# Probabilities as the stationary operand, an unselected phase for the first token tiles, and wider score banks and FFN blocks

## The chip, the cores and the metric

One core of a Trainium2 chip runs the whole program. The metric is the device time of one execution in microseconds (us), as the median of several runs of the same program.

## What is computed

Attention with a choice of key chunks, and a feed-forward block (FFN) behind it. Batch 4, 8 heads, 768 tokens, head size 64; FFN over 3072 tokens, 512 to 2048 to 512, weights in float32.

```python
k_min, k_max = chunk minima and maxima of k       # 24 chunks of 32 keys
ub = sum(max(q * k_min, q * k_max), axis=-1)      # one bound per query and chunk
ub = where(causal by chunk, ub, -1e9)
top_chunks = argsort(ub)[..., -6:]                # six chunks per query
scores = where(chosen and causal, q @ k.T / 8, -1e9)
x = softmax(scores) @ v                           # (3072, 512), heads side by side
h = maximum(x @ w_in, 0)
out = (h * h) @ w_out
```

The first 128 tokens of a batch see four chunks at most, fewer than six, so that nothing is left out for them.

## The kernel before

A *pair* is two heads of one batch; there are 16 pairs, four per batch. Everything is held in SBUF as bf16. GpSimd issues the loads (`load_qk`, `load_v`: two heads of 768 tokens each; `load_w_in`, `load_w_out`), SyncE the stores.

`stage_a` prepares a pair: TensorE (PE) transposes k and q one head at a time (line 188, 64 columns of the array each), VectorE copies them into `kqc` and `qsc` (L198), reduces chunk maxima and minima (L203), and splits q into its positive and negative parts (L215, L216). `selection` multiplies these into the bounds `ub` (L228, L230), finds the sixth largest (L239), marks the chunks that are not chosen (`selb`, L240), turns the marks with PE (`sT`, L248) and copies them below q (L253). The score product then has 88 rows: 64 of q and k, and 24 that subtract 32768 where a chunk is not chosen.

`stage_b` works on a pair and a block of 384 queries. For each key tile of 128 and each head it makes transposed scores `ps` (keys x queries, L378), ScalarE takes the exponential into `e` (L382), and GpSimd zeroes the upper triangle of diagonal tiles (`affine_select`, L385). `values` uses v as the stationary operand, with 64 columns of ones beside its 64 columns, and moves up to 384 columns of `e` through it (L344): half of the output rows are the sums. `finish` takes their reciprocal as exp(-ln) on ScalarE (L358, L361) and VectorE multiplies into `xT` (L368), which is already transposed for the FFN.

Four pairs complete a block of 384 tokens. `ffn_units` cuts its FFN into 16 units `up` (four matmuls of 384 columns into `ph`, L287; relu on ScalarE, L292; square on VectorE, L294) and 12 units `down` (four matmuls of 512 columns into `py`, L301; the last copies out, L306, and stores). `run_ffn` places them between score tiles at a rate per column (`pace`), and a block's units run beside the attention of the next block; after the last pair 144 FFN matmuls stand alone.

The table `phases` lists, block by block, stage A, stage B and the loads; `aside` spreads stage A between key tiles. From the program so written the framework's scheduler makes each engine's list: it moves instructions that are free to go ahead of others, so that the lists differ from the order of the code. Each engine runs its list strictly in order. PSUM is split into one bank for transposes and bounds (`pst`), three for scores, two for values, two for the FFN.

## Time and profile before

| | |
|---|---|
| median of 3 runs | 325.76 us (325.62 to 326.14) |
| span of the profiled execution, first to last instruction | 324.3 us |
| PE busy, 2096 matmuls | 294.6 us, 91% |
| ScalarE (ACT) busy, 548 instructions | 221.1 us, 68% |
| VectorE (DVE) busy, 619 | 207.9 us, 64% |
| GpSimd (POOL) busy, 254 | 110.0 us, 34% |
| chain that ended last, by engine | PE 66%, DVE 17%, ACT 7% |

No time of its own is given for the profiled execution; its span is 1.5 us below the median of the runs. Busy time is the union of the records. A matmul's record lasts from its issue until its result is out, several overlap, and so the busy share of PE says little of how many columns it could still take; the distance between two starts says more.

### The profile page before, as it was taken

To read this page: it belongs to the slowest core of one execution; us is meant where nothing else is said; L and a number is where in the kernel's file an instruction comes from. 1 tells how busy PE (TensorE), PEld (TensorE's weight loads), DVE (VectorE), ACT (ScalarE), POOL (GpSimd) and SP (SyncE) were. 2 spreads that over 40 slices of the span, in tenths; PEclk is the share of its full clock that TensorE was granted. 3 is DMA by queue.
4 is the path that set the end of the run, shared out by engine and by line. 5 is a ranking of instruction groups with operands and counts; after the bars stand their busy time and mean duration, and the time that the engine had idled before them with its cause. 6 is when DMAs were issued, how large, how long until landed. Compare 5 with 4: busy or idle time off the path is not lost.

```text
span 324.3 us, 6103 instructions
## 1 busy us (share of the span) xinstructions
PE 294.6 (91%) x2096; PEld 158.9 (49%) x2096; DVE 207.9 (64%) x619; ACT 221.1 (68%) x548; POOL 110.0 (34%) x254
## 2 busy tenths in 40 slices
PE   1577699999998999999999999999999999999995
PEld 0233345554454555555455545554455555554542
DVE  6775678997799877995576487993675214421420
ACT  6367377984477486887579667787489679973731
POOL 8954754892224733223323212120123211210000
PEclk9999999999999999999999999999999999999999
DMA  9999999999503971333140000000100000001001
GB/s 76 173 179 192 108 199 154 136 145 114 92 0 26 136 102 35 25 24 26 66 59 2 32 34 34 0 2 1 67 33 0 34 33 32 2 0 65 35 32 65
DMA packets 81642, 20.86 MB, mean 64 GB/s; under 512 B 75108, under 2 KB 78028, under 8 KB 81612
## 3 DMA queue, kind: packets, MB, share of 16 engines
q0 software_dynamic: 77616, 13.63, 53.3%
q1 hardware_dynamic: 3996, 6.85, 5.7%
q8 instruction: 16, 0.26, 0.3%
q14 instruction: 14, 0.11, 0.1%
HBM read 27.26 MB, written 6.29 MB: 103 GB/s over the span
## 4 chain that ended last, share of the span: by engine, by line
PE 66%; DVE 17%; ACT 7%; issue 3%; POOL 3%; DMA 2%; POOLq 0%; ACTq 0%
PE py L301 23%; PE ph L287 18%; PE ps L378 9%; DVE xT L368 3%; ACT rc L358 3%; DVE qsc L198 3%; PE kT L188 2%; DMA kn<-in_k_dram 2%; DVE kr L203 2%; PE sT L248 2%; ACT e L382 2%; ACT ht L292 1%; PE qT L188 1%; ACT rc L361 1%; DVE qp L215 1%
## 5 line engine op out<-in xcount | busy, mean ns | idle before, releaser
L382 ACT ACTIVATE e<-ps 128x384 bf16<-128x384 f32 (+2 forms) x288 | 111.4, 431 | 34.7 <-PE ps L378 33.2
L385 POOL TENSOR_SCALAR_AFFINE_SELECT e<-e 128x128 bf16<-128x128 bf16 x192 | 57.0, 305 | 167.4 <-ACT e L382 165.8
L287 PE MATMUL ph<-xT,w_in_sb 128*128 128x384 bf16 x512 | 106.3, 329 | 3.0 <-ACT ht L292 2.7
L378 PE MATMUL ps<-qsc,kqc 88*128 88x384 bf16 (+2 forms) x288 | 72.9, 306 | 3.2 <-ACT e L382 2.7
L292 ACT ACTIVATE ht<-ph 128x384 bf16<-128x384 f32 x128 | 63.8, 505 | 15.4 <-PE ph L287 13.1
L287 PEld LDWEIGHTS <-w_in_sb 128*128 128x128 bf16 x512 | 48.2, 98 | 37.5 <-issue 12.6
L344 PEld LDWEIGHTS <-vo 128*128 128x128 bf16 x288 | 28.4, 101 | 21.6 <-issue 6.2
L378 PEld LDWEIGHTS <-kqc 88*128 88x128 bf16 x288 | 27.4, 101 | 19.4 <-issue 3.3
L198 DVE COPY kqc<-kT 64x768 bf16<-64x768 bf16 (+1 forms) x40 | 19.0, 474 | 25.7 <-PE kT L188 25.3
L203 DVE TENSOR_REDUCE kr<-kT 128x24 bf16<-128x768 bf16 (+1 forms) x40 | 30.4, 792 | 0.3
L306 ACT COPY ob<-py 128x512 f32<-128x512 f32 x24 | 14.1, 586 | 22.0 <-PE py L301 21.8
L253 DVE COPY qsc<-sT 24x640 bf16<-24x640 bf16 (+2 forms) x40 | 16.7, 417 | 4.1 <-PE sT L248 3.3
L85 POOL DMA_DIRECT2D vo<-in_v_dram x16 | 16.5, 1039 | 6.9 <-PE ps L378 6.9
L188 PE MATMUL kT<-ident,kn 128*64 128x128 bf16 x192 | 10.9, 239 | 8.7 <-DMA kn<-in_k_dram 8.2
L198 DVE COPY qsc<-qT 64x768 bf16<-64x768 bf16 (+1 forms) x32 | 16.1, 503 | 3.7 <-PE qT L188 3.3
L75 POOL DMA_DIRECT2D kn<-in_k_dram x16 | 16.6, 1036 | 2.0 <-PE ps L378 1.2
L361 ACT ACTIVATE rc<-rc 128x384 f32<-128x384 f32 x32 | 16.5, 515 | 0.1
L75 POOL DMA_DIRECT2D qn<-in_q_dram x16 | 16.4, 1027 | 0.2
L188 PEld LDWEIGHTS <-kn 128*64 128x64 bf16 x192 | 6.8, 116 | 16.6 <-DMA kn<-in_k_dram 9.0
L248 PE MATMUL sT<-ident,selb 128*128 128x128 bf16 x80 | 8.5, 232 | 4.7 <-DVE selb L240 4.3
L188 PE MATMUL qT<-ident,qn 128*64 128x128 bf16 x192 | 10.3, 237 | 1.3 <-DMA qn<-in_q_dram 1.0
L188 PEld LDWEIGHTS <-qn 128*64 128x64 bf16 x192 | 6.6, 115 | 9.2 <-issue 5.7
(646 smaller groups left out, 470.7 us busy)
## 6 DMA issues: line engine op xcount, KB each, us to landing
out_dram<-ob SPq DMA_DIRECT2D x24, 256.0 KB
kn<-in_k_dram POOLq DMA_DIRECT2D x16, 192.0 KB, 5.2
qn<-in_q_dram POOLq DMA_DIRECT2D x16, 192.0 KB, 5.5
vo<-in_v_dram POOLq DMA_DIRECT2D x16, 192.0 KB, 5.3
w_out_sb<-in_moe_w_out_dram POOLq DMA_DIRECT2D x1, 2048.0 KB, 15.7
w_in_sb<-in_moe_w_in_dram POOLq DMA_DIRECT2D x1, 1536.0 KB, 11.4
kqc<-kqc SPq DMA_DIRECT2D x15, 36.0 KB
w_in_sb<-in_moe_w_in_dram POOLq DMA_DIRECT2D x1, 512.0 KB, 9.4
```

Source lines behind the costliest of these rows:

```text
L75: nc.gpsimd.dma_start(out=nat[nm, b][:, h:h + 2].rearrange("p h j d -> p (h j) d"), in_=src[b, h:h + 2].rearrange("h (j p) d -> p (h j) d" ...
L188: nc.tensor.matmul(pt[D * hh:D * hh + D, 128 * j:128 * (j + 1)], lhsT=nat[nm, b][:, 2 * hp + hh, n0 * HT + j], rhs=ident, is_transpose=Tru ...
L198: nc.vector.tensor_copy(ops[s][hh][0:D, cols], pt[rows])
L203: nc.vector.tensor_reduce(kr[:, mm], pt.rearrange("d (c j) -> d c j", j=CH), axis=AX.X, op=op)
L287: nc.tensor.matmul(ph, lhsT=w_in_sb[:, ki, 128 * f:128 * (f + 1)], rhs=xT[:, ki], start=(ki == 0), stop=(ki == NKI - 1))
L292: nc.scalar.activation(ht, ph, ACT.Relu)
L301: nc.tensor.matmul(py, lhsT=h2[f][:, 128 * t:128 * (t + 1)], rhs=w_out_sb[:, f, :], start=(f == 0), stop=(f == NFI - 1))
L344: nc.tensor.matmul(hold["av"][hh][:, off:], lhsT=vo[b % 2].rearrange("p h n d -> p (h n d)")[:, c0:c0 + 2 * D], rhs=es[hh][:, off:], start ...
L361: nc.scalar.activation(rc, rc, ACT.Exp, scale=-1.0)
L378: nc.tensor.matmul(ps[:, off:], lhsT=kq[s][hh][:, 128 * j:128 * (j + 1)], rhs=qs[s][hh][:, q0 + off:q1], start=True, stop=True)
L382: nc.scalar.activation(e[:, off:], ps[:, off:], ACT.Exp, scale=scale)
L385: nc.gpsimd.affine_select(out=e[:, off:off + 128], in_=e[:, off:off + 128], compare_op=ALU.is_ge, fill=0.0, base=0, channel_multiplier=-1, ...
```

## The change

The queries of the first tile of every batch leave the selection. A new phase at the start (`first_transpose`, `first_scores`, `first_values`) handles the tile (0, 0) of all heads of all four batches: 64-row scores without marks, exponential, triangle, values. Its result `x_first` is an FFN block of 512 tokens. The other 640 tokens of a batch are one block, whose `up` units go in halves of 320 columns. There are five blocks instead of eight.

Scores are packed: per head and pair five PSUM banks of 512 columns (`BANKS`), each filled by two products of the 15 tiles below and the five on the diagonal; one exponential covers a bank. `values` takes each 128 x 128 tile of `e` as the stationary operand and moves 65 columns of v through it (64 and a column of ones), so that the output has queries as rows; `normalise` divides by the 65th column on VectorE. Hence x must be transposed for the FFN: `turn`, four PE transposes and a VectorE copy per tile.

k and q of both heads are transposed at once (128 columns of the array), q without its first tile, and q is copied by ScalarE. Loads go by token tile over all eight heads. At the end of every batch the queue `behind` and the remaining FFN units are drained. Four sets of `kqc`/`qsc` instead of eight; six buffers of `e` (of 512) instead of twelve (of 384).

```diff
+    QC = 128 * NS
+    VW = 80
+    NSET = 4
+    LAG = 3
...
-    epool = ctx.enter_context(tc.tile_pool(name="epool", bufs=12))
-    hpool = ctx.enter_context(tc.tile_pool(name="hpool", bufs=NFI + 8))
+    epool = ctx.enter_context(tc.tile_pool(name="epool", bufs=LAG + 3))
+    hpool = ctx.enter_context(tc.tile_pool(name="hpool", bufs=NFI + 6))
...
-    psav = ctx.enter_context(tc.tile_pool(name="psav", bufs=1, space=PSUM))
+    psav = ctx.enter_context(tc.tile_pool(name="psav", bufs=2, space=PSUM))
...
+    def load_first(nm, b0, b1):
...
+            out=dst.rearrange("p b h d -> p (b h) d"),
+            in_=SRC[nm][b0:b1, :, 0:128].rearrange("b h p d -> p (b h) d"))
...
+    def load_rest(nm, b, j):
...
+        nc.gpsimd.dma_start(
+            out=nat[nm, b][:, j - 1, :, 0:D],
+            in_=SRC[nm][b, :, 128 * j:128 * (j + 1)].rearrange("h p d -> p h d"))
...
+    load_first("k", 0, 2)
     ident = consts.tile([128, 128], BF16, tag="ident")
     make_identity(nc, ident)
-    load_qk(0, "q")
-    load_qk(1)
+    load_first("q", 0, 2)
+    load_first("v", 0, 2)
+    load_first("k", 2, 4)
+    load_first("q", 2, 4)
+    load_first("v", 2, 4)
+    load_w_in(0, 4)
...
+    for nm in "kq":
+        for j in range(1, NT):
+            load_rest(nm, 0, j)
+    load_w_in(4, 8)
...
+    def causal(e, n):
+        nc.gpsimd.affine_select(
+            out=e, in_=e, compare_op=ALU.is_ge, fill=0.0, base=0,
+            channel_multiplier=-1, pattern=[[0, n], [1, 128]])
+    def normalise(av, n, x):
+        rc = work.tile([128, NS], F32, tag="rc", name="rc")
+        nc.vector.reciprocal(rc[:, 0:n], av[:, :, D])
+        nc.vector.tensor_mul(
+            x, av[:, :, 0:D],
+            rc[:, 0:n].unsqueeze(2).to_broadcast([128, n, D]))
+    x_first = work.tile([128, B, d_model], BF16, tag="x0", name="x0", bufs=1)
+    t_first = {}
+    e_first = {}
+    def first_transpose(b):
+        pt = pst.tile([128, 2, NP, 128], BF16, tag="tp", name="T0")
+        for i, nm in enumerate("kq"):
+            for hp in range(NP):
+                nc.tensor.matmul(pt[:, i, hp], lhsT=key_tile(nm, b, hp, 0),
+                                 rhs=ident, is_transpose=True,
+                                 start=True, stop=True)
+        t_first[b] = work.tile([128, 2, NP, 128], BF16, tag="t0", name="t0")
+        nc.vector.tensor_copy(t_first[b], pt)
+    def first_scores(b):
+        t = t_first.pop(b)
+        es = []
+        for hh in range(2):
+            rows = slice(D * hh, D * hh + D)
+            ps = pss.tile([128, NP, 128], F32, tag="ps", name="ps0")
+            for hp in range(NP):
+                nc.tensor.matmul(ps[:, hp], lhsT=t[rows, 0, hp],
+                                 rhs=t[rows, 1, hp], start=True, stop=True)
+            e = epool.tile([128, NP, 128], BF16, tag="e", name="e0")
+            nc.scalar.activation(e, ps, ACT.Exp, scale=scale)
+            causal(e, NP)
+            es.append(e)
+        e_first[b] = es
+    def first_values(b):
+        es = e_first.pop(b)
+        for hh in range(2):
+            av = psav.tile([128, NP, D + 1], F32, tag="av", name="av0")
+            for hp in range(NP):
+                nc.tensor.matmul(av[:, hp], lhsT=es[hh][:, hp],
+                                 rhs=value_tile(b, 2 * hp + hh, 0),
+                                 start=True, stop=True)
+            normalise(av, NP, x_first[:, b].rearrange(
+                "p (hp hh d) -> p hp hh d", hh=2, d=D)[:, :, hh])
...
+        pt = pst.tile([128, S], BF16, tag="tp", name="kT")
+        for j in range(NT):
+            nc.tensor.matmul(pt[:, 128 * j:128 * (j + 1)],
+                             lhsT=key_tile("k", b, hp, j), rhs=ident,
+                             is_transpose=True, start=True, stop=True)
...
+        pt = pool.tile([128, QC], BF16, tag=tag, name="qT")
+        for j in range(1, NT):
+            nc.tensor.matmul(pt[:, 128 * (j - 1):128 * j],
+                             lhsT=key_tile("q", b, hp, j), rhs=ident,
+                             is_transpose=True, start=True, stop=True)
...
+        for hh in range(2):
+            nc.scalar.copy(qss[0:D, s, hh], pt[D * hh:D * hh + D])
...
+    def ffn_units(x, rows, parts):
...
+        def turn(t):
+            pt = psf.tile([128, NKI, 128], BF16, tag="ff", name="xt")
+            for ki in range(NKI):
+                nc.tensor.matmul(pt[:, ki], lhsT=x[:, t, 128 * ki:128 * (ki + 1)],
+                                 rhs=ident, is_transpose=True,
+                                 start=True, stop=True)
+            nc.vector.tensor_copy(xT[:, :, 128 * t:128 * (t + 1)], pt)
...
-                    rhs=xT[:, ki],
+                    rhs=xT[:, ki, c0:c1],
...
+        for t in range(n):
+            units.append((0.25, lambda t=t: turn(t)))
         for f in range(NFI):
-            units.append((tb, lambda f=f: up(f)))
+            for c0, c1 in parts:
+                units.append(((c1 - c0) / 512, lambda f=f, c0=c0, c1=c1:
+                              up(f, c0, c1)))
...
+    BANKS = [
+        ([(0, 1, 2), (1, 1, 2)], (2, 3)),
+        ([(2, 2, 1), (0, 3, 3)], (0, 1)),
+        ([(4, 4, 1), (1, 3, 3)], (0, 1)),
+        ([(5, 5, 1), (3, 3, 3)], (0, 2)),
+        ([(4, 5, 1), (2, 3, 3)], None),
+    ]
...
+    def values(p, hh, i, e, x):
...
+        for n, (j, t0, nt) in enumerate(BANKS[i][0]):
+            for t in range(t0, t0 + nt):
+                nc.tensor.matmul(
+                    av[:, t - 1], lhsT=e[:, 128 * c:128 * (c + 1)],
+                    rhs=value_tile(b, 2 * hp + hh, j),
+                    start=(i == 0 and c == 0), stop=(i == len(BANKS) - 1),
+                    skip_group_check=True)
...
+        if i == len(BANKS) - 1:
+            h = 2 * hp + hh
+            normalise(held.pop("av"), NS, x[:, :, D * h:D * (h + 1)])
...
+        for hh in range(2):
+            for i, (runs, diagonal) in enumerate(BANKS):
+                ps = pss.tile([128, 512], F32, tag="ps", name="ps")
+                c = 0
+                for j, t0, nt in runs:
+                    nc.tensor.matmul(
+                        ps[:, 128 * c:128 * (c + nt)],
+                        lhsT=kqs[:, s, hh, 128 * j:128 * (j + 1)],
+                        rhs=qss[:, s, hh, 128 * (t0 - 1):128 * (t0 - 1 + nt)],
+                        start=True, stop=True)
+                    c += nt
+                e = epool.tile([128, 512], BF16, tag="e", name="e")
+                nc.scalar.activation(e, ps, ACT.Exp, scale=scale)
+                if diagonal:
+                    d0, d1 = diagonal
+                    causal(e[:, 128 * d0:128 * d1].rearrange(
+                        "p (n j) -> p n j", j=128), d1 - d0)
+                run_ffn()
+                behind.append(lambda p=p, hh=hh, i=i, e=e, x=x:
+                              values(p, hh, i, e, x))
+                if len(behind) > LAG:
                     behind.pop(0)()
...
+    first_transpose(0)
+    first_transpose(1)
+    first_scores(0)
+    first_transpose(2)
+    first_scores(1)
+    first_values(0)
+    first_transpose(3)
+    first_scores(2)
+    first_values(1)
+    first_scores(3)
+    first_values(2)
+    first_values(3)
+    ffn.extend(ffn_units(x_first, [S * b for b in range(B)], [(0, 512)]))
...
+    loads(6)
+    aside.append((0, stage_a(0)))
+    for p in range(B * NP):
+        b, hp = divmod(p, NP)
+        if hp == 0:
+            x = work.tile([128, NS, d_model], BF16, tag="x", name="x")
+            pace["rate"] = sum(u[0] for u in ffn) / (10 * NP)
+        finish_a(p)
+        if p + 1 < B * NP:
+            aside.append((p + 1, stage_a(p + 1)))
+        loads(8)
+        stage_b(p, x)
+        if hp == NP - 1:
+            while behind:
+                behind.pop(0)()
+            while ffn:
+                ffn.pop(0)[1]()
+            pace["due"] = 0.0
+            ffn.extend(ffn_units(
+                x, [S * b + 128 * t for t in range(1, NT)],
+                [(0, QC // 2), (QC // 2, QC)]))
```

On GpSimd, this is the start of the list before (`kn`, `qn`, `vo` are k, q, v of two heads).

```order
L75 DMA kn<-in_k_dram 128x12x64
masks.py:197 MEMSET ident 128x128
L75 DMA qn<-in_q_dram 128x12x64
...
L85 DMA vo<-in_v_dram 128x12x64 x2
L385 AFFINE_SELECT e<-e 128x128 x12
L156 DMA w_in_sb<-in_moe_w_in_dram 128x4x1536
```

And now (`k_86`, `q_87`, `v_88` are first tiles, `e_178` to `e_288` their probabilities, `kn`, `qn`, `vn` the other tiles).

```order
L74 DMA k_86<-in_k_dram 128x16x64
...
L103 DMA w_in_sb<-in_moe_w_in_dram 128x4x512
L151 MEMSET ubmask 128x120
...
L86 DMA qn<-in_q_dram 128x8x64 x5
L103 DMA w_in_sb<-in_moe_w_in_dram 128x4x512
L168 AFFINE_SELECT e_178<-e_178 128x512
...
L168 AFFINE_SELECT e_288<-e_288 128x512
L83 MEMSET vn 128x40
L86 DMA vn<-in_v_dram 128x8x64 x2
L103 DMA w_in_sb<-in_moe_w_in_dram 128x4x1024
L86 DMA vn<-in_v_dram 128x8x64 x3
L108 DMA w_out_sb<-in_moe_w_out_dram 128x8x512 x2
L86 DMA kn<-in_k_dram 128x8x64 x5
L86 DMA qn<-in_q_dram 128x8x64
L168 AFFINE_SELECT e<-e 128x128 x3
```

Before, the first select stood behind 13 loads; now 18 loads stand ahead of the first tiles' selects, and 14 more between these and the first select of pair 0.

On ScalarE, the start of the list before, and now.

```order
L196 COPY qsc<-qT 64x384 x4
L382 ACTIVATE e<-ps 128x384 x2
L382 ACTIVATE e<-ps 128x256 x2
L382 ACTIVATE e<-ps 128x128 x2
L196 COPY qsc<-qT 64x384 x2
```

```order
L205 ACTIVATE e_280<-ps_275 128x512
L205 ACTIVATE e_288<-ps_283 128x512
L254 COPY qsc<-qT 64x640 x2
L405 ACTIVATE e<-ps 128x512 x6
L320 ACTIVATE ht<-ph 128x512
L254 COPY qsc<-qT 64x640 x2
L320 ACTIVATE ht<-ph 128x512 x7
L405 ACTIVATE e<-ps 128x512 x7
```

The first relu of the FFN (`ht`) now stands behind eight exponentials of the first tiles, the q copies of pair 0 and six of its banks.

On PE, the place of the first score product before (`kn` transposes of pair 2 and bounds of pair 1 around it), and the end of the first phase now (`e_178` holds probabilities of the first tiles, `qn` is the rest of q of pair 0).

```order
L188 MATMUL kT<-ident,kn 64x128
L378 LDWEIGHTS kqc
L378 MATMUL ps<-qsc,kqc 128x384
L228 LDWEIGHTS qp
L228 MATMUL ub<-kbd,qp 128x48
```

```order
L227 MATMUL kT<-ident,kn 128x128
L246 LDWEIGHTS qn
L246 MATMUL qT<-ident,qn 128x128
...
L215 LDWEIGHTS e_178
L215 MATMUL av_216<-v_88,e_178 128x65
```

The transposes of k and q of pair 0 stand behind the first tiles' scores and ahead of their values, where before pairs 0 to 2 went through their first halves one after the other. The first `ph` product now stands behind nine banks of `ps`.

## Rows read from the trace of the kernel before

**Rows 1.** Busy time by stretches: us, then each engine (count), clock, DMA share, GB/s.
```profile
0.00:45.00 45.00, 27.45 (x167) 13.42 (x168) 30.59 (x107) 24.84 (x56) 30.06 (x61) 1.00 1.53 150
45.00:150.00 105.00, 100.91 (x830) 55.30 (x829) 92.01 (x282) 76.70 (x196) 50.14 (x97) 1.00 1.00 84
150.00:290.00 140.00, 135.63 (x947) 75.23 (x946) 78.49 (x213) 106.22 (x272) 29.81 (x97) 1.00 0.11 26
290.00:324.30 34.30, 30.62 (x156) 14.98 (x154) 6.84 (x18) 13.34 (x26) 0.00 (x0) 1.00 0.12 47
```

**Rows 2.** The chain that ended last, from 296 us: start us, length us, what.
```profile
299.08 0.65 PE ph L287 x4
...
299.76 10.53 PE ph L287 x60
310.29 10.37 PE py L301 x48
...
320.68 0.58 ACT ob L306
```

**Rows 3.** PE in order of time, two places past 49 us: start us, length us, what.
```profile
49.96 0.22 PE L344 MATMUL av_709<-e,vo 128*128 128x128 bf16 x1
50.02 0.22 PE L344 MATMUL av_710<-e,vo 128*128 128x128 bf16 x1
...
93.11 0.53 PE L188 MATMUL qT<-ident,qn 128*64 128x128 bf16 x12
93.57 2.51 PE L287 MATMUL ph<-xT,w_in_sb 128*128 128x384 bf16 x13
...
96.24 0.19 PE L228 MATMUL ub<-kbd,qp 128*128 128x48 bf16 x1
...
96.47 0.18 PE L230 MATMUL ub<-kbd,qm 128*128 128x48 bf16 x1
```

**Rows 4.** Groups by line and form: busy us, mean ns | idle before.
```profile
L287 PE MATMUL ph<-xT,w_in_sb 128*128 128x384 bf16 x512 | 106.3, 329 | 3.0 <-ACT ht L292 2.7
...
L344 PEld LDWEIGHTS <-vo 128*128 128x128 bf16 x288 | 28.4, 101 | 21.6 <-issue 6.2
...
L75 POOL DMA_DIRECT2D kn<-in_k_dram x16 | 16.6, 1036 | 2.0 <-PE ps L378 1.2 <-POOLq L468 0.8
```

**Rows 5.** PE's groups of the first 45 us alone.
```profile
L378 PE MATMUL ps<-qsc,kqc 88*128 88x384 bf16 (+2 forms) x32 | 11.0, 410 | 0.2 <-ACT e L382 0.2
L287 PE MATMUL ph<-xT,w_in_sb 128*128 128x384 bf16 x12 | 5.2, 518 | 0.1
```

**Rows 6.** PE in order of time at 22 us and at 46 us.
```profile
22.10 0.53 PE L344 MATMUL av_336<-e,vo 128*128 128x384 bf16 x1
22.42 0.53 PE L344 MATMUL av_337<-e,vo 128*128 128x384 bf16 x1
...
46.01 0.34 PE L378 MATMUL ps<-qsc,kqc 88*128 88x384 bf16 x1
46.18 0.49 PE L287 MATMUL ph<-xT,w_in_sb 128*128 128x384 bf16 x2
```

**Rows 7.** ScalarE in order of time at 55 us.
```profile
54.89 0.51 ACT L382 ACTIVATE e<-ps 128x384 bf16<-128x384 f32 x1
55.26 0.53 ACT L292 ACTIVATE ht<-ph 128x384 bf16<-128x384 f32 x1
```

**Rows 8.** Three more stretches, columns as in rows 1.
```profile
0.00:5.00 5.00, 0.00 (x0) 0.00 (x0) 3.48 (x15) 2.23 (x3) 3.81 (x10) 1.00 0.64 41
40.00:50.00 10.00, 9.64 (x62) 5.03 (x63) 7.55 (x28) 6.84 (x18) 4.70 (x9) 1.00 1.22 196
55.00:75.00 20.00, 19.67 (x167) 11.10 (x166) 18.59 (x61) 16.92 (x45) 18.09 (x27) 1.00 2.13 136
```

**Rows 9.** VectorE in order of time, one selection from 88 us on.
```profile
88.30 1.00 DVE L253 COPY qsc<-sT 24x640 bf16<-24x640 bf16 x2 [0.28 <-PE sT L248]
...
95.29 0.49 DVE L215 TENSOR_SCALAR qp<-qT 128x640 bf16<-128x640 bf16 x1
```

More of the change, by code (lines that the diff above doesn't have):

```diff
@@ L104 @@
-    selb = [selbs[:, s] for s in range(NSET)]
     def kq_rows(i):
@@ new lines, in stage_a @@
+        for j in range(NT):
[3 more added lines that the diff above has]
+        for hh in range(2):
+            nc.vector.tensor_copy(kqs[0:D, s, hh], pt[D * hh:D * hh + D])
+        kr = work.tile([128, 2, NC], BF16, tag="kr", name="kr")
+        for mm, op in ((0, ALU.max), (1, ALU.min)):
+            nc.vector.tensor_reduce(
+                kr[:, mm], pt.rearrange("d (c j) -> d c j", j=CH),
+                axis=AX.X, op=op)
@@ L227, in selection @@
+        qp = work.tile([128, QC], BF16, tag="qp", name="qp")
+        qm = work.tile([128, QC], BF16, tag="qm", name="qm")
+        nc.vector.tensor_scalar_max(qp, pt, 0.0)
+        nc.vector.tensor_scalar_min(qm, pt, 0.0)
+        for hh in range(2):
+            nc.scalar.copy(qss[0:D, s, hh], pt[D * hh:D * hh + D])
+        yield
+        ub = pst.tile([128, NS, 2, NC], F32, tag="tp", name="ub")
+        for i in range(NS):
             tile_cols = slice(128 * i, 128 * (i + 1))
-            nc.tensor.matmul(ub[:, i], lhsT=qp[:, tile_cols], rhs=kbd[s][:, 0],
+            nc.tensor.matmul(ub[:, i], lhsT=qp[:, tile_cols], rhs=kbds[:, s, 0],
@@ L236, in selection @@
         m8 = work.tile([128, NS, 2, 8], F32, tag="m8", name="m8")
-        for i in range(m):
+        for i in range(NS):
             for hh in range(2):
@@ L256 @@
-    ffn = []
-    xTs = {}
-    nunits = NFI + (QB // 128) * (NFI // 4)
-    behind = []
-    KEEP = 8
-    LAG = 2
-    aside = []
-    def beside(n):
-        while n and aside:
-            if next(aside[0][1], aside) is aside:
-                aside.pop(0)
-            else:
-                n -= 1
-    def finish_a(p, half):
-        while any(p == x[0][0] and half in x[0][1] for x in aside):
-            beside(1)
-    left = {tb: NP for tb in range(n_tok // QB)}
-    def ffn_units(tb):
-        units = []
-        h2 = [None] * NFI
-        t0 = QB * tb
-        xT = xTs.pop(tb)
-        def up(f):
-            ph = psf.tile([128, QB], F32, tag="ff", name="ph")
+            nc.vector.tensor_copy(qss[D:KC, s, hh], sT[32 * hh:32 * hh + NC])
@@ new lines, with beside, finish_a, up @@
+    aside = []
+    def beside():
+        if aside and next(aside[0][1], aside) is aside:
+            aside.pop(0)
+    def finish_a(p):
+        while any(p == x[0] for x in aside):
+            beside()
+    ffn = []
+    def ffn_units(x, rows, parts):
+        n = len(rows)
+        xT = work.tile([128, NKI, 128 * n], BF16, tag="xT", name="xT")
+        h2 = [None] * NFI
+        units = []
+        def turn(t):
[5 more added lines that the diff above has]
+            nc.vector.tensor_copy(xT[:, :, 128 * t:128 * (t + 1)], pt)
+        def up(f, c0, c1):
+            ph = psf.tile([128, c1 - c0], F32, tag="ff", name="ph")
@@ L450, with run_ffn @@
-    while behind:
-        behind.pop(0)()
+    def run_ffn():
+        pace["due"] += pace["rate"]
+        while ffn and pace["due"] >= ffn[0][0]:
+            cost, unit = ffn.pop(0)
+            pace["due"] -= cost
+            unit()
+    BANKS = [
[5 rows of a table added]
+    ]
+    behind = []
+    held = {}
+    def values(p, hh, i, e, x):
+        b, hp = divmod(p, NP)
+        if i == 0:
+            held["av"] = psav.tile([128, NS, D + 1], F32, tag="av", name="av")
+        av = held["av"]
+        c = 0
[6 more added lines that the diff above has]
+                    skip_group_check=True)
+                c += 1
+        if i == len(BANKS) - 1:
+            h = 2 * hp + hh
+            normalise(held.pop("av"), NS, x[:, :, D * h:D * (h + 1)])
@@ new lines @@
+    first_transpose(0)
[11 more added lines that the diff above has]
+    ffn.extend(ffn_units(x_first, [S * b for b in range(B)], [(0, 512)]))
+    later = []
+    for j in range(1, NT):
+        later.append(lambda j=j: load_rest("v", 0, j))
+        if j == 2:
+            later.append(lambda: load_w_in(8, NFI))
@@ new lines, with loads @@
+    later.append(lambda: load_w_out(0, 8))
+    later.append(lambda: load_w_out(8, NFI))
+    for b in range(1, B):
+        for nm in "kqv":
+            for j in range(1, NT):
+                later.append(lambda nm=nm, b=b, j=j: load_rest(nm, b, j))
+    def loads(n):
+        for _ in range(min(n, len(later))):
+            later.pop(0)()
+    loads(6)
[19 more added lines that the diff above has]
+                [(0, QC // 2), (QC // 2, QC)]))
```

294 lines of the change are left out of this document (60 added, 234 removed).

## The prediction

> **What bounds the kernel now.** I read the stretches first, then the order of TensorE's instructions in time, then the groups by form. The four stretches show TensorE (PE) busy through most of the middle, but a record runs from issue to result [rows 1]; what it needs is better read from the distance between two starts. On the chain that ended last, 48 matmuls of 512 columns take 10.37 us, 0.216 each, and a pure run of four with 384 columns 0.65, 0.162 each [rows 2]. Two value products of 128 columns, each with a weight load of its own, start 0.055 apart (0.06 as rounded), and the upper-bound products of 48 columns, also one load each, nine steps in 0.23 us, 0.025 each [rows 3]. Twelve half-width transposes fill 93.11 to 93.57, 0.038 each [rows 3]. So the cost is 0.42 ns per column, with a floor at 0.025 us.
>
> With the counts of rows and loops [rows 4] PE's work before is: up 512 x 0.162 = 82.9; down 24 tiles x 16 x 0.216 = 82.9; scores 160 x 0.162 + 64 x 0.109 + 64 x 0.055 = 36.4; values the same 36.4; transposes of k and q 384 x 0.038 = 14.6; mask transposes 80 x 0.055 = 4.4; upper bounds 160 x 0.025 = 4.0. Sum 261.6 of a span of 324.3, so 62.7 us are not work. The runs' median, 325.76, is 1.5 above this span; I add that 1.5 at the end.
>
> Where the 62.7 lie: up to 45 us only 12 up matmuls and 32 scores have run [rows 5], with 24 values and 66 half transposes about 11.7 us of work: 33 us lost. Part of that is the clock: at 22 us two value products of 384 columns start 0.32 apart, which is 1.2 GHz, though the clock column prints 1.00 there [rows 1, 6]; at 46 us a score and an up matmul of 384 columns start 0.17 apart [rows 6], so the rise to 2.4 GHz lies between, when scores and up matmuls had begun to run densely. In the last stretch, 64 up, 83 down and six values make 29.4 of 34.3 us; 3.6 of the rest lie behind the last matmul (copy 0.58 and the store) [rows 2]. That leaves 220.5 of work in the 245 us between 45 and 290: 24.5 lost, 11% on the work.
>
> **The change, part by part.** *Value products.* 672 products (16 pairs x 2 heads x 20 tiles, and 32 first ones) of 65 columns replace 288 wide ones. No row has 65 columns: the bounds are the 48-column step, 0.025, and the 128-column step, 0.055; by 0.42 ns per column 65 come to 0.030, near the lower end. 672 x 0.030 = 20.2 for 36.4: **-16.2** (-19.6 to +0.6). The rule that speaks against this comes after the sum.
> *Transposes.* 208 of full width x 0.055 = 11.4 for 14.6, and 96 new ones of x for the FFN, 5.3: **+2.1**.
> *Scores.* Per head and pair four of 128, two of 256, four of 384 columns: 1.086 x 32 = 34.8, and 32 first ones 1.8: **+0.2**. *Up.* 64 x 0.216 + 512 x 0.136 = 83.4: **+0.5**. Down, bounds and masks stay. New work: **248.2**, 13.4 less.
> *ScalarE and VectorE.* Back to back, exps of 384 start 0.37 apart [rows 7], so 512 take about 0.49; 168 of them replace 288, the Ln/Exp chain goes and 24 more q copies come. VectorE loses those copies and the 64 multiplies into xT. Both stay below PE per pair: ten exps, eight relus of 0.31, two copies of about 0.68, 1.25 stores of 0.48 make 9.3 us, against 13.4 of PE work in a pair of batches 1 to 3. I cost them at nothing there; PE covers them.
>
> *The start* decides how much of the 13.4 is kept. 205 KB moved in the first 5 us and small packets move at 136 GB/s, weights at 196 [rows 8], so transfers begin near 3.5 us. Ahead of batch 0's selection now stand six first-tile loads of 256 KB (11.6 us), 512 KB of w_in (2.7) and ten loads of 128 KB for the rest of k and q (9.6): the last lands at about 28. GpSimd's issues (1.04 us for 12 rows, about 0.9 for 8 [rows 4]) end near 20 and don't set this. In PE's order the five q transposes stand ahead of the first values and of every FFN matmul, so PE waits there until 28. Then VectorE's list runs to the mask copies: qp and qm about 0.9, the pair of mask copies 1.0 [rows 9], bound, ten maxima and compare 1.7, eight normalisations between them at about 0.45, one xT copy 0.4: 7.6, with transposes and hand-offs 9. The first score bank starts at 37. ScalarE's list has six exps ahead of the first relu, 6 x 0.49, and PE's has nine banks ahead of the first up matmul: the FFN begins near 41. The FFN on the first tiles, though ready data, hence doesn't fill the start. By 41 PE has done 64 first-tile matmuls, 17 transposes, 32 first values, 16 x transposes, nine banks and the bounds and masks, 8.8 us; until 45 at 1.2 GHz another 2.2. So 11.0 at 45 us, against 11.7 before: the start is a wash.
>
> *From 45 on* 237.2 us of work are left. 35.8 are the last block, which stands alone: 20 transposes (1.1), 128 up (17.4), 80 down (17.3); before, 144 matmuls stood behind the last value product. The other 201.4 get an allowance for waits. Before it was 11% there; 160 score banks hand over to ScalarE instead of 288, the value banks double and the selection is spread over the pairs, so I take **9%** (5 to 12): 219.5. Each of three batch ends drains its queue and turns x before the next block: last exp, normalisation, transpose and copy, of which about 1.2 us stay open: 3.5. At the end the same chain has no cover, 3.0; and up halves run at the pace of two PSUM buffers. Before, 60 up matmuls, 15 units, took 10.53 us [rows 2], 0.70 per unit for 0.65 of work: a buffer's cycle is 0.65, the relu's 0.49 and 0.26 of hand-offs, and two buffers halve it. With 0.54 and 0.44 a half takes 0.62 for 0.54, 32 times 0.08: 2.6.
>
> Sum: 45 + 219.5 + 3.5 + 35.8 + 5.6 + 3.6 = 313.0, and 1.5: **314 us**, -3.5%.
>
> **Weight loads against the rows.** In rows 3 a 128-column product with its own load takes 0.055 and a 48-column one 0.025. The Trainium skill, "TensorE: Matmul & The Clock Gate", section "Back-to-back issue gap", says that a stream of load and matmul pairs sustains about 81 ns at 128 columns. By that rule, 672 value products would cost at least 54.4 us, and the sum would be 348. Rows 3 contradict it here.
>
> **Rivals.** (1) *Slower: the load of the probabilities sets the pace of the value products.* Each stationary tile is used once, and a load's record lasts 0.10 [rows 4]; if it is not hidden under 65 columns, 672 x 0.10 = 67 instead of 20, or 361 us. It decides from 0.048 per product, where the 11.8 us gained are gone. Against it: 48 columns hide theirs at 0.025. 6%.
> (2) *A later start or a standing wait in pair 0.* On GpSimd the first selects of pair 0 stand behind 14 issues (13 us) that follow the first tiles' selects, near 45; if the 35 up matmuls ahead of the values don't cover that, or q lands later, all behind moves one for one: 5 to 18 us, 319 to 332. 20%; it ends above the old time from 11.8 us on.
> (3) *The middle waits less* (5%), or the selection of pair 0 slips between the normalisations: 8 to 14 us less, 300 to 306. 20%.
> (4) *It doesn't do what it says: the unselected phase would fill the start.* This is what I expect not to happen; if it did, some 6 us more would be gained, which lies in (3)'s reach.
>
> **Numbers.** Forecast 52% with its own range 307 to 320, (3) 20%, (2) 20%, (1) 6%, the rest 2%. About 0.2% is what a measurement tells from no change, 325.1 to 326.4. Faster: 52 + 20 + 9 of (2) = 0.81; same 0.04; slower 0.15. The 8-in-10 range takes the forecast, most of (3) and the lower half of (2): 301 to 327.
>
> **What would show it.** Right: value products at 0.025 to 0.035 from start to start; the first up matmul at 38 to 44 us with about 11 us of work done by 45; last up halves at 0.6 each and the last block about 45 us from the last value product to the end. Wrong: value products at 0.05 or more; the first up matmul before 30 or after 50; PE waiting for `e` on GpSimd in pair 0; lost time in the middle outside 5 to 12% of its work.

## The result and the profile after

The changed kernel takes **316.16 us** (median of 4 runs, 315.94 to 317.10); the kernel before, run beside it on the same chip, 325.95. The ratio is 0.971, 95% interval 0.968 to 0.974: 2.9% faster, for a forecast of 314. The profiled execution spans 314.4 us. A few executions of the runs below took 490 us and more; they stand in no median and no ratio here.

Stretches of the changed kernel (columns as in [rows 1]), cut where the work changes: start, loads still running, middle, end.

```profile
0.00:45.00 45.00, 24.08 (x193) 15.31 (x195) 19.73 (x62) 13.45 (x23) 35.53 (x52) 1.00 1.58 140
45.00:105.00 60.00, 52.14 (x514) 31.36 (x521) 40.18 (x125) 39.70 (x73) 47.91 (x83) 0.97 1.78 146
105.00:270.00 165.00, 160.30 (x1557) 103.22 (x1571) 110.61 (x371) 118.76 (x238) 28.59 (x88) 1.00 0.07 24
270.00:314.40 44.40, 39.70 (x244) 21.95 (x244) 13.05 (x39) 17.50 (x38) 0.00 (x0) 1.00 0.10 36
```

The second one stands out. PE is busy in 52.14 of 60 us there; before, it was busy in 100.91 of 105 [rows 1]. GpSimd is busy in 47.91 of the 60, with DMA at 146 GB/s, and the clock is below 1.

The chain of waits that ended last, from 268 us on:

```profile
268.34 0.12 PE av L381 x4
...
270.41 0.50 PE av L381 x16
...
273.74 19.65 PE ph L315 x128
293.39 0.34 PE py L330
...
293.78 10.74 PE py L330 x49
...
304.57 6.22 PE py L330 x28
...
310.86 0.58 ACT ob L335
```

Four value products take 0.12 us and sixteen 0.50, 0.030 to 0.031 each, as forecast (0.030); before, a product of 128 columns took 0.055 [rows 3]. The last block takes 2.83 us from the last value product (270.91) to the first up product, then 19.65 for the up and 17.40 for the down products, and 3.6 behind the last matmul: 43.5 us for a forecast of 45.0.

The start. VectorE and PE in order of time, changed kernel:

```profile
28.67 0.49 DVE L251 TENSOR_SCALAR qp<-qT 128x640 bf16<-128x640 bf16 x1 [0.97 <-PE qT L246]
...
34.48 0.42 DVE L176 TENSOR_TENSOR x<-av,rc 128x256 bf16<-128x256 f32 x1
...
35.37 1.00 DVE L282 COPY qsc<-sT 24x640 bf16<-24x640 bf16 x2
...
40.50 0.41 DVE L310 COPY xT<-xt 128x512 bf16<-128x512 bf16 x1
```

```profile
35.91 1.04 PE L398 MATMUL ps<-qsc,kqc 88*128 88x256 bf16 x4
...
38.79 2.25 PE L398 MATMUL ps<-qsc,kqc 88*128 88x128 bf16 x10
...
41.21 2.75 PE L315 MATMUL ph<-xT,w_in_sb 128*128 128x512 bf16 x11
```

q's transposes are done just ahead of 28.67 (forecast 28), the first score bank comes at 35.91 (37) and the first up product at 41.21 (41). The ten score products from 38.79 on, five banks or 2560 columns in 2.25 us, still go near 1.2 GHz. The eleven up products in 2.75 us, the last one's record being 0.38, start 0.24 apart for 512 columns each, so by then the clock is at 2.4 GHz, which the forecast had only from 45 us on. Counted with the prediction's prices, PE's work by 45 us is 32 scores and 32 transposes of the first tiles (3.5 us), 36 values (1.1), 16 turns of x (0.9), 18 scores (1.9), 27 transposes and 20 bound products (2.0) and 12 up (2.6): 12.0 us, for a forecast of 11.0, and 11.7 in the kernel before.

So the three parts of the sum came out at 45 + 225.9 + 43.5 = 314.4 us. The middle, from 45 to the last value product, had been put at 223.0; 200.4 us of it are work (248.2 - 12.0 - 35.8), 25.5 lost.

Where it is lost. GpSimd in order of time from 32 us on, changed kernel (in brackets the idle time ahead, and what ended it):

```profile
32.61 0.77 POOL L103 DMA_DIRECT2D w_in_sb<-in_moe_w_in_dram  x1
33.35 2.66 POOL L86 DMA_DIRECT2D vn<-in_v_dram  x3
35.95 1.81 POOL L108 DMA_DIRECT2D w_out_sb<-in_moe_w_out_dram  x2
37.68 1.83 POOL L86 DMA_DIRECT2D kn<-in_k_dram  x2
42.20 2.62 POOL L86 DMA_DIRECT2D kn<-in_k_dram  x3 [2.69 <-DMA w_in_sb<-in_moe_w_in_dram]
44.80 0.90 POOL L86 DMA_DIRECT2D qn<-in_q_dram  x1
45.67 1.61 POOL L168 TENSOR_SCALAR_AFFINE_SELECT e<-e 128x128 bf16<-128x128 bf16 x5
49.81 0.90 POOL L86 DMA_DIRECT2D qn<-in_q_dram  x1 [2.52 <-DMA w_out_sb<-in_moe_w_out_dram]
...
54.88 0.89 POOL L86 DMA_DIRECT2D qn<-in_q_dram  x1 [2.50 <-DMA w_out_sb<-in_moe_w_out_dram]
55.78 0.42 POOL L168 TENSOR_SCALAR_AFFINE_SELECT e<-e 128x256 bf16<-128x256 bf16 x1
...
69.44 1.79 POOL L86 DMA_DIRECT2D qn<-in_q_dram  x2
71.19 0.63 POOL L168 TENSOR_SCALAR_AFFINE_SELECT e<-e 128x128 bf16<-128x128 bf16 x2
```

A load's issue doesn't only take 0.9 us: three of them stand for 2.5 to 2.7 us until a transfer of weights has ended, and what is behind them in GpSimd's list stands too. In each of the three, the transfer waited for is that of the load issued eight places earlier, as the rows let one count (42.20 waits for the load issued at 32.61, 49.81 and 54.88 for the two of 35.95). The kernel before, with 51 loads instead of 71, has no wait of a load for a transfer. Whether the program or the chip holds the issue, no run here tells. PE at the same time, and the stretch from 56 to 60 us:

```profile
53.27 0.38 PE L315 MATMUL ph<-xT,w_in_sb 128*128 128x512 bf16 x1
56.26 0.62 PE L381 MATMUL av<-vn,e 128*128 128x65 bf16 x8 [2.61 <-POOL e L168]
...
71.60 0.23 PE L381 MATMUL av<-vn,e 128*128 128x65 bf16 x2 [1.06 <-POOL e L168]
```

```profile
56.00:60.00 4.00, 3.52 (x24) 2.35 (x26) 2.24 (x6) 1.86 (x4) 4.00 (x7) 0.57 2.43 155
```

From 56 to 60 us, after PE had stood for 2.61 us, the granted clock was 0.57 on the mean, so mostly the lower of its two levels, 1.2 GHz. The waits of the whole stretch from 45 to 105 us (total us, times, longest), changed kernel:

```profile
PEld L381 <- POOL e L168: 9.1, 9, 3.1
...
PE av L381 <- POOL e L168: 6.3, 7, 2.6
```

PE's loads of `e` and the products behind them are the ones that wait, on GpSimd and on nothing else of weight; the two lines count much of the same time. Of the seven waits of products only the first, in pair 0, stands behind an issue that was held. The six others (0.3 to 1.1 us, 3.7 in all) are in pairs 2 to 4, and each stands behind issues that merely take their 0.9 us each, as the select of 71.19 behind those of 69.44. The chain of waits that ended last goes through GpSimd's issues and selects, and one transfer of w_out behind which they stood, most of the way from 29 to 100 us.

### The profile page after: what moved, and what is told of

It is laid out like the page before. It is cut to its first block, busy times and chain, and to the rows that moved or that the text cites. A ratio compares the mean times of both kernels' runs of the same rounds, so it can differ in the third digit from the quotient of the medians.

```text
span 314.4 us, 6653 instructions
## 1 busy us (share of the span) xinstructions
PE 276.2 (88%) x2503; PEld 171.8 (55%) x2528; DVE 183.6 (58%) x595; ACT 189.4 (60%) x370; POOL 112.0 (36%) x222
## 4 chain that ended last, share of the span: by engine, by line
PE 48%; POOL 17%; DMA 11%; DVE 11%; ACT 8%; issue 3%; ACTq 0%; POOLq 0%
PE ph L315 18%; PE py L330 16%; DMA w_out_sb<-in_moe_w_out_dram 6%; POOL vn L86 5%; PE ps L398 5%; DVE kr L234 5%; ACT qsc L254 4%; PE av L381 4%; POOL qn L86 4%; DMA w_in_sb<-in_moe_w_in_dram 4%; POOL e L168 3%; DVE kqc L231 3%; POOL kn L86 3%; ACT ht L320 2%; DMA qn<-in_q_dram 2%
## 5 line engine op out<-in xcount | busy, mean ns | idle before, releaser
L405 ACT ACTIVATE e<-ps 128x512 bf16<-128x512 f32 x160 | 92.4, 601 | 51.9 <-PE ps L398 50.3
L315 PE MATMUL ph<-xT,w_in_sb 128*128 128x320 bf16 (+1 forms) x572 | 98.6, 307 | 1.2 <-issue 0.2
L168 POOL TENSOR_SCALAR_AFFINE_SELECT e<-e 128x128 bf16<-128x128 bf16 (+2 forms) x136 | 47.3, 356 | 143.1 <-ACT e L405 140.5
L330 PE MATMUL py<-w_out_sb,h 128*128 128x512 bf16 x363 | 94.0, 378 | 0.9
L320 ACT ACTIVATE ht<-ph 128x320 bf16<-128x320 f32 (+1 forms) x144 | 64.7, 457 | 25.2 <-PE ph L315 16.1
L398 PE MATMUL ps<-qsc,kqc 88*128 88x128 bf16 (+1 forms) x320 | 61.8, 278 | 0.5
L323 DVE TENSOR_TENSOR h<-ht 128x320 bf16<-128x320 bf16 (+1 forms) x144 | 47.2, 339 | 22.7 <-ACT ht L320 21.6
L381 PEld LDWEIGHTS <-e 128*128 128x128 bf16 x640 | 38.3, 98 | 30.8 <-POOL e L168 9.6
L330 PEld LDWEIGHTS <-h 128*128 128x128 bf16 x384 | 36.5, 97 | 29.0 <-issue 0.2
L381 PE MATMUL av<-vn,e 128*128 128x65 bf16 x480 | 38.6, 194 | 6.7 <-POOL e L168 6.3
L231 DVE COPY kqc<-kT 64x768 bf16<-64x768 bf16 x32 | 17.7, 553 | 15.9 <-PE kT L227 15.4
L86 POOL DMA_DIRECT2D kn<-in_k_dram x20 | 18.1, 918 | 2.7 <-DMA w_in_sb<-in_moe_w_in_dram 2.7
```

What stands on the lines that cost most here:

```text
L86: nc.gpsimd.dma_start(out=nat[nm, b][:, j - 1, :, 0:D], in_=SRC[nm][b, :, 128 * j:128 * (j + 1)].rearrange("h p d -> p h d"))
L168: nc.gpsimd.affine_select(out=e, in_=e, compare_op=ALU.is_ge, fill=0.0, base=0, channel_multiplier=-1, pattern=[[0, n], [1, 128]])
L231: nc.vector.tensor_copy(kqs[0:D, s, hh], pt[D * hh:D * hh + D])
L315: nc.tensor.matmul(ph, lhsT=w_in_sb[:, ki, 128 * f:128 * (f + 1)], rhs=xT[:, ki, c0:c1], start=(ki == 0), stop=(ki == NKI - 1))
L320: nc.scalar.activation(ht, ph, ACT.Relu)
L323: nc.vector.tensor_mul(h2[f][:, c0:c1], ht, ht)
```

## Experiments

**Theory A**: in pairs 0 to 4 the selects stand behind load issues that are themselves held up, which costs most of what PE loses ahead of value products. **Rivals**: the way from a score through exp and select to the value product is too long for three banks anywhere (B); loads or VectorE are what is late (C). Further runs take the other terms of the forecast one at a time. Medians and ratios to the kernel before, each run beside it:

| label | us | ratio (95%) | against 316.16 |
|---|---|---|---|
| e1_wide_v | 323.45 | 0.990 (0.988 to 0.992) | +7.3 |
| e2_loads4 | 315.71 | 0.966 (0.964 to 0.969) | -0.4 |
| e5_lag5 | 311.27 | 0.952 (0.950 to 0.955) | -4.9 |
| e3_start | 315.87 | 0.967 (0.964 to 0.969) | -0.3 |
| e7_mask | 308.55 | 0.947 (0.945 to 0.949) | -7.6 |
| e8_mask_start | 309.01 | 0.948 (0.946 to 0.950) | -7.2 |
| e4_last | 312.39 | 0.961 (0.956 to 0.965) | -3.8 |
| e6_noflush | 313.76 | 0.962 (0.959 to 0.965) | -2.4 |
| e9_all3 | 304.38 | 0.933 (0.930 to 0.937) | -11.8 |
| e11_all3_turn | 305.33 | 0.937 (0.934 to 0.940) | -10.8 |
| e10_all3_lag5 | 307.05 | 0.942 (0.938 to 0.945) | -9.1 |
| e12_pst2 | 300.78 | 0.922 (0.918 to 0.925) | -15.4 |

The last column compares medians of different sessions, in which the kernel before stood between 325.9 and 326.7; it is good to about 1 us, and by the ratios the differences come out from 0.3 us less negative (e4_last) to 1.3 us more (e5_lag5).

### e1_wide_v: the price of a value product

```diff
-    VW = 80
+    VW = 112
+    VN = D + 33
...
-        return t[:, h, 0:D + 1]
+        return t[:, h, 0:VN]
```

`av` and the columns of ones are widened alike; to make room the output has two buffers instead of three.

> Every value product reads 97 columns instead of 65 (32 more columns of ones behind each head's values, whose results nobody reads). Theory, columns set the pace: start to start goes from 0.029 to 0.040 us, 672 x 32 x 0.42 ns = +9.0 us of TensorE work, of which 5 to 9 reach the end: 321 to 325 us for 316.2. Rival, the load of the probabilities sets the pace: products stay at 0.029 and the time at 316 +- 1.

Its chain of waits has the last sixteen products at

```profile
277.72 0.71 PE av L385 x16
```

for 0.50: (0.71 - 0.50) / 16 / 32 = 0.41 ns per column added. 672 products make 8.8 us of work, of which some 6 to 7 reach the end (7.3 by the medians, 6.1 by the ratios). Columns set the pace, not the load of the probabilities, which is the same in both: rival (1) of the prediction is out. The Trainium skill, "TensorE: Matmul & The Clock Gate", section "Back-to-back issue gap", gives about 81 ns for sustained pairs of load and product at 128 columns, and N / 2.4 + 2.5 ns for isolated ones (by estimate 29.6 at 65). It has no figure for pairs at 65 columns; the prediction's 348 took that of 128. Here streams of such pairs run at 55 ns with 128 columns [rows 3] and at 30 to 31 ns with 65, near the isolated formula, and the measurement decides.

### e2_loads4, e5_lag5, e7_mask: what the value products wait for

e2_loads4 has one line:

```diff
-        loads(8)
+        loads(4)
```

> GpSimd issues 4 loads per pair instead of 8 ahead of each pair's selects. Theory A, DMA issues that wait for earlier weight transfers stand ahead of the selects and cost most of the 10.7 us that TensorE loses ahead of value products, nearly all from 45 to 105 us: 306 to 311 us, the waits for e on GpSimd from 50 to 100 us fall below 3 us. Rival B, the way from score over exp and select to value product is too long for three banks whatever GpSimd issues: 315 to 317 us, the same waits. Rival C, the loads are needed that early: later pairs wait for k, q or v, 317 to 325 us.

Hardly anything was gained (0.4 us by the medians, 1.6 by the ratios), and the edit did not do what it says. The last of the v loads is issued at the same time as in the changed kernel (view of one tile, changed kernel and then this one: durations in ns, first and last start):

```profile
L86 POOL DMA_DIRECT2D vn<-in_v_dram x20: 881/910/926, 30.8 to 99.4; - x20
```

```profile
L86 POOL DMA_DIRECT2D vn<-in_v_dram x20: 881/900/926, 30.1 to 99.7; - x20
```

Written four a pair, the loads would last into pair 11; the trace shows them all issued by 101 us. Few of them wait for a result of the program, and the framework's scheduler moves what is free ahead of the rest. The waits for GpSimd stayed too, in this kernel over the same 60 us:

```profile
PE av L381 <- POOL e L168: 8.3, 10, 1.9
...
PEld L381 <- POOL e L168: 12.8, 13, 2.4
```

This run tells A and B apart not at all.

e5_lag5:

```diff
-    LAG = 3
+    LAG = 5
```

> Value products follow their scores five banks later instead of three, with two more exp buffers. Theory A (stalled issues ahead of the selects, up to 5 us at once): five banks are some 6.5 us of TensorE work for 4, so part of the stalls is covered, 2 to 5 us less, 311 to 314 us. Rival B (the chain is too long for three banks everywhere): the waits ahead of value products go in all pairs, 6 to 10 us less, 306 to 310 us. If neither holds, 316 +- 1, and the drains at the batch ends get 0.5 us longer each.

The edit also raises the buffers of `e` from six to eight. It gained 4.9 us by the medians, the upper end of A's range, and 6.2 by the ratios, the lower end of B's; the time doesn't decide between them, the waits do. From 45 to 105 us the same waits are

```profile
PE av L381 <- POOL e L168: 2.2, 3, 1.4
...
PEld L381 <- POOL e L168: 2.9, 4, 1.5
```

and behind 105 us there was next to nothing of them to take away in the changed kernel (0.5 us up to 255). That speaks for A and against B, but for a cover, not for the cause.

e7_mask takes the select itself off GpSimd in pairs 0 to 4 (`NDVE` is 5, `tri` a constant triangle of ones and zeros):

```diff
-                    causal(e[:, 128 * d0:128 * d1].rearrange(
-                        "p (n j) -> p n j", j=128), d1 - d0)
+                    ed = e[:, 128 * d0:128 * d1].rearrange(
+                        "p (n j) -> p n j", j=128)
+                    if p < NDVE:
+                        nc.vector.tensor_mul(
+                            ed, ed, tri.unsqueeze(1).to_broadcast(
+                                [128, d1 - d0, 128]))
+                    else:
+                        causal(ed, d1 - d0)
```

> In pairs 0 to 4 the causal triangle is applied by VectorE, as a product with a constant triangle of ones, and no longer by GpSimd's select, so no probability bank of these pairs waits behind a DMA issue; everything else is as in the changed kernel. Theory A (issues that stall on earlier weight transfers stand ahead of the selects): the 10.7 us that TensorE loses ahead of value products shrink to 3 or less, 306 to 310 us. Rival B (the chain from score to value product is too long for three banks, whatever does the select): VectorE's product takes 0.15 to 0.3 us, as the select does, and the time stays at 314 to 317 us. Rival C (VectorE, at 7 to 9 tenths there, becomes the wait): 316 to 320 us.

308.55: in A's range and in neither rival's. Stretches 45 to 105 and 56 to 60 us of this kernel, and what is left of the wait:

```profile
45.00:105.00 60.00, 57.27 (x574) 35.64 (x573) 49.36 (x182) 43.81 (x84) 34.83 (x43) 1.00 1.76 143
...
56.00:60.00 4.00, 3.69 (x39) 1.88 (x37) 2.86 (x18) 3.96 (x9) 4.00 (x6) 1.00 2.41 157
```

```profile
PE av L388 <- DVE e L418: 0.2, 1, 0.2
```

PE is busy in 57.27 of the 60 us instead of 52.14, the clock stays up, and the loads still come at 143 GB/s. GpSimd's issues still stand for weights (one for 4.38 us); nothing on PE's path stands behind them. So it is shown that the selects' place behind the issues costs these 7.6 us (8.1 by the ratios). That the holding of issues costs most of it, as theory A has it, is not shown: behind a held issue stood one wait of PE, 2.61 us and the slow clock after it, and the six later ones behind issues that weren't held; this edit takes both away at once.

### e3_start, e8_mask_start: what sets the start

```diff
-    load_first("k", 2, 4)
-    load_first("q", 2, 4)
-    load_first("v", 2, 4)
-    load_w_in(0, 4)
...
             load_rest(nm, 0, j)
+    load_first("k", 2, 4)
+    load_first("q", 2, 4)
+    load_first("v", 2, 4)
+    load_w_in(0, 4)
```

and `stage_a(0)` goes ahead of `first_transpose(2)`.

> Loads of the first tiles of batches 2 and 3 and the first w_in block go behind those of batch 0's other k and q tiles, and the selection of pair 0 stands ahead of the first tiles of batches 2 and 3 on TensorE. Theory, the start is set by the loads ahead of batch 0's q (three of 256 KB and 512 KB of w_in, 8.5 us of transfer): the last q tile lands near 20 instead of 28, the first score bank comes at 30 to 33 instead of 35.9, the first up product at 36 to 40, and 2 to 6 us are gained: 310 to 314 us. Rival, VectorE's list (two more first transposes' copies and the normalisations) or the loads of the first tiles, now last, set the start: first score bank within 1 us of 35.9, 315 to 318 us.

The transfer and the first bank came earlier as the theory expected, and next to nothing was gained (0.3 us by the medians, 1.5 by the ratios): the time is the rival's, though not its sign, a first bank near 35.9. VectorE in order of time, then the views of `ps` and `ph` (durations, first and last start), this kernel:

```profile
20.22 0.49 DVE L251 TENSOR_SCALAR qp<-qT 128x640 bf16<-128x640 bf16 x1 [1.02 <-PE qT L246]
...
28.94 0.48 DVE L282 COPY qsc<-sT 24x640 bf16<-24x640 bf16 x1
...
39.09 0.41 DVE L176 TENSOR_TENSOR x<-av,rc 128x256 bf16<-128x256 f32 x1
```

```profile
L398 PE MATMUL ps<-qsc,kqc x18: 264/406/527, 28.8 to 39.1; 88*128 88x128 bf16 x7, 88*128 88x384 bf16 x7, 88*128 88x256 bf16 x4
```

```profile
L315 PE MATMUL ph<-xT,w_in_sb x49: 376/379/627, 41.2 to 60.0; 128*128 128x512 bf16 x49
```

q is there 8.4 us earlier and the banks start 7 us earlier, but the first tiles' last normalisation comes at 39.09 instead of 34.48, and the up products at 41.2 as in the changed kernel. GpSimd reached pair 0's first selects at 45.4 us here and at 45.67 in the changed kernel, so the gain could also have been lost there. That is what e8_mask_start asks; it puts e7's and e3's edits together.

> The triangle of pairs 0 to 4 on VectorE, and also the earlier selection of pair 0 (first tiles of batches 2 and 3 loaded and computed behind it). The earlier selection alone changed nothing, although pair 0's mask copies ended at 29.4 instead of 36.4 us. Theory A: its gain was lost to the same wait, since GpSimd reached the first selects of pair 0 at 45 us in both; with the selects off GpSimd both gains add: 3 to 6 us below the triangle's run alone. Rival: the transfers (first tiles of batches 2 and 3, v of batch 0, w_in) now come last and set the start of the FFN and of the value products: within 1.5 us of the triangle's run alone.

309.01 for 308.55: theory A's addition failed, and the time is the rival's. That what was moved back now comes last, as the rival has it, is not shown: no trace here tells.

### e4_last, e6_noflush: the end and the batch ends

```diff
-            ph = psf.tile([128, c1 - c0], F32, tag="ff", name="ph")
+            pool, tag = (pss, "ps") if last and c0 else (psf, "ff")
+            ph = pool.tile([128, c1 - c0], F32, tag=tag, name="ph")
```

and the same for every second turn of x (`xt`).

> In the last block alone, up halves and transposes of x alternate between the two FFN banks and the three score banks, which are idle then. Theory (the prediction's two-buffer pace): of the 4.6 us that TensorE loses from 270 us on, the 2.0 between up halves and 1 of the 1.7 between transposes of x go: 312.5 to 314.5 us for 316.2. Rival (ScalarE's relu or VectorE's square sets the pace of the halves): 315.5 to 316.5 us.

312.39, 0.1 below the theory's range, and in the chain of this kernel

```profile
271.92 17.67 PE ph L317 x128
```

for 19.65: 0.138 per product, which is its price (0.136), so that the two buffers had cost 2.0 us. Neither ScalarE nor VectorE limits the halves. From the last value product to the first up product it is 2.21 us instead of 2.83; the two make 2.6 of what was gained, and what the rest is stays open.

```diff
-            while behind:
-                behind.pop(0)()
-            while ffn:
-                ffn.pop(0)[1]()
-            pace["due"] = 0.0
-            ffn.extend(ffn_units(
+            if b == B - 1:
+                while behind:
+                    behind.pop(0)()
+                while ffn:
+                    ffn.pop(0)[1]()
+            pending.append(ffn_units(
...
+                if pending and pace["n"] == LAG:
+                    ffn.extend(pending.pop())
```

> No drain at the ends of batches 0 to 2: the next FFN block starts three banks into the next batch, and the value products in flight stay in the queue. Theory (the prediction's 1.2 us per batch end): 3 to 4 us less, 312 to 313.5 us. Rival (the drains are covered, since the next pair's scores and selection stand behind them and are ready): 315.5 to 317 us.

-2.4 us (-3.1 by the ratios): 0.8 to 1.0 per batch end. The drains cost something, a little less than the theory's 1.2; the rival is out. (Where the next block begins, its pace is set anew, which the cut above leaves out.)

### e9_all3, e11_all3_turn, e10_all3_lag5: together

e9_all3 has the edits of e7_mask, e4_last and e6_noflush.

> Three edits together: the triangle of pairs 0 to 4 on VectorE (alone -7.6 us), no drains at the batch ends (alone -2.4), five buffers in the last block (alone -2.5). Theory, the three take away waits of different stretches (45 to 105 us, batch ends, the end): they add to -12.5, 303.7 us (302.5 to 305). Rival, with fewer waits ScalarE and VectorE become the bound in the middle and half of it is lost: 306 to 309 us.

304.38, within the range: -11.8, where the expectation added up -12.5 and the medians of the table give -13.8. The three add up but for some 2 us at most, about what differences between sessions leave open.

e11_all3_turn adds

```diff
+    for _ in range(B):
+        ffn.pop(0)[1]()
```

behind the first block's `ffn_units`, which makes the turns of x at once.

> The three edits, and the transposes of x for the first FFN block stand ahead of pair 0's banks instead of among them, so that on VectorE the last copy into xT goes ahead of pair 1's k copies and reductions (2.9 us in the changed kernel, from 37.6 to 40.5). Theory (VectorE's list, not the loads, sets where the FFN starts, as the run with earlier loads left the FFN at 43 us): first up product near 38 instead of 41 us, 1.5 to 3 us less than with the three edits alone. Rival (the mask copies come later by the moved copies, or what is gained is lost at the slow clock): within 0.8 us of the three edits alone.

The first up product came as early as expected, and 305.33 says it was worth nothing. `ph` and `ps` in e11, then `ps` in e9:

```profile
L324 PE MATMUL ph<-xT,w_in_sb x51: 376/378/634, 36.7 to 59.9; 128*128 128x512 bf16 x51
```

```profile
L408 PE MATMUL ps<-qsc,kqc x14: 221/318/527, 38.0 to 44.2; 88*128 88x128 bf16 x5, 88*128 88x384 bf16 x5, 88*128 88x256 bf16 x4
```

```profile
L408 PE MATMUL ps<-qsc,kqc x20: 263/421/527, 35.2 to 40.7; 88*128 88x128 bf16 x8, 88*128 88x384 bf16 x8, 88*128 88x256 bf16 x4
```

The banks moved from 35.2 back to 38.0, while the up products, first at 41.8 in e9, moved ahead by 5 us. As in e3_start, one of the two streams that PE needs was moved ahead and the other did not follow: there the up products stayed where they were and the first tiles' last normalisation came 4.6 us later, here the banks fell back by 2.8.

e10_all3_lag5 has e9's edits and `LAG = 5`.

> The three edits with value products five banks behind their scores instead of three. Theory A (what five banks gave alone, 4.9 us, was cover for GpSimd's stalled issues, and the triangle on VectorE has taken these away already): within 1 us of the three edits alone. Rival B (part of it is the ordinary chain from score to value product in all pairs): 2 to 4 us less than the three edits alone.

2.7 us slower than e9, which neither expected. Rival B is out, and five banks have nothing left to cover, as A says, but they cost something, which A doesn't have. In this kernel the same constant also sets at which bank the next FFN block begins and at what rate the first one runs, so this run doesn't say which of them costs it. That stays open.

### e12_pst2: the rest of the middle

```diff
-    pst = ctx.enter_context(tc.tile_pool(name="pst", bufs=1, space=PSUM))
-    pss = ctx.enter_context(tc.tile_pool(name="pss", bufs=3, space=PSUM))
+    pst = ctx.enter_context(tc.tile_pool(name="pst", bufs=2, space=PSUM))
+    pss = ctx.enter_context(tc.tile_pool(name="pss", bufs=2, space=PSUM))
```

on top of e9's edits.

> The three edits, and one PSUM bank moved from the score banks (three to two) to the selection's transposes (one to two). From 105 to 255 us the three edits still lose some 10% of TensorE's time, and the largest waits there that are not a matmul's own are for VectorE at the selection: qT's transposes wait until the reductions have read kT's bank. Theory (the selection's single bank holds TensorE up): about 0.5 us less in each of 16 pairs and in the first phase, 6 to 10 us less than the three edits alone, 295 to 299 us. Rival (two score banks make TensorE wait for ScalarE's exps instead): 305 to 312 us.

300.78, the fastest here: 3.6 us less than e9, half of what the theory gave. The waits from 105 to 255 us, e9 and then e12:

```profile
PE qT L253 <- DVE kr L241: 1.9, 6, 0.4
...
PEld L253 <- DVE kr L241: 3.7, 6, 0.7
```

```profile
PE ub L269 <- DVE qm L259: 2.1, 6, 0.4
...
PEld L269 <- DVE qm L259: 3.5, 6, 0.7
```

q's transposes no longer wait for the reductions of k, but the next product of the selection now waits for VectorE's split of q, about as long: a good part of the wait moved on to the next step. PE is busy in 146.29 of these 150 us instead of 144.01. The rival's wait for exps didn't appear there.

## Why the prediction was right, and where it was not

**Right, step by step.** *Value products*: 0.030 forecast, 0.030 to 0.031 measured, and e1_wide_v shows that the price goes by columns; choosing the lower bound by its nearness to the 48-column row was sound. *The start is a wash*: 12.0 us of work by 45 for 11.0 forecast and 11.7 before; q, the first bank and the first up product came within 1.1 us of their times. *The last block*: a half at 19.65 / 32 = 0.61 us for 0.62, the pace of two buffers 2.0 us by e4_last for 2.6, the chain with its 20 transposes of x 2.83 for 4.1 (3.0 and 1.1), 3.6 behind the last matmul; in all 43.5 for 45.0. *Rival (1)* fell by the first row.

**Right for another reason than given.** The middle was to lose 9% evenly, 18.1 us, and 3.5 at the batch ends: 21.6. It lost 25.5. Of these, 7.6 are GpSimd's selects behind load issues (e7_mask), 2.4 to 3.1 the batch ends (e6_noflush), and the rest, some 15, is 7.5% of the work, less than the allowance; e12_pst2, with a second bank for the selection, gave back 3.6 of it. So **rival (2)**, given 20%, happened in part, inside a total that looks like the forecast, and its sign came, PE waiting for `e` on GpSimd in pair 0. Its price of 5 to 18 was for pair 0 alone, though, where PE stood once, for 2.61 us; the 7.6 are those of pairs 0 to 4 together. These were offset by a better middle, a shorter last block and a clock that rose before 45 us, and that the sum came out within 1.4 us of the profiled span (313.0 for 314.4) is in part luck. The place was foretold well (first selects near 45, measured 45.67), the mechanism only by half. The prediction counted 14 issues at 0.9 each, once. It did not see that an issue can be held until a weight transfer ends, nor that issues go on between the selects until 100 us, so that the wait came back in pairs 2 to 4.

**What failed.** The step "the last lands at about 28 ... PE waits there until 28", as what *decides* the start: q at 20 us (e3_start) changes nothing. PE needs two streams there, pair 0's banks and the first tiles' x, and VectorE's list carries both. Moving one of them ahead left the time within some 1.5 us of what it was (e3_start, e11_all3_turn). What exactly would shorten both is open. The assumption of 1.2 GHz until 45 us was off by some 4 us, worth the 1 us of work.

The median lies 1.8 us above the profiled span, where 1.5 was added.

## What to carry to other kernels

Before pricing an instruction on an engine that also issues loads, look for the issues ahead of it in that engine's list, and at whether they are themselves held by earlier transfers: here 0.9 us of issue became 3.4 when a weight load stood eight places ahead of it. Where a scheduler writes the lists, check in the trace that an edit moved what it names; a load that depends on nothing isn't delayed by writing it later. A forecast can be right by offsetting errors, so the terms should be checked one by one, each by an experiment that moves only that term.

## What the runs showed that was not expected

GpSimd's issue of a load stood until an earlier weight transfer had ended, 2.5 to 2.7 us in the changed kernel and up to 4.92 in e3_start, and that transfer was each time the one issued eight loads before. A stall of PE of 2.61 us was followed by 4 us at a mean granted clock of 0.57; without the stall (e7_mask) it stayed at 1.00 in the same 4 us. What was forecast and is now measured: a value product of 65 columns with a stationary operand of its own takes 0.030 us, and 32 columns more cost 0.41 ns each.
